# Strassen second layer from group 18 on in the first superblock, its operands prepared during the MLP

## The chip, the cores and the metric

The kernel runs on one core of one Trainium2 chip. The metric is the device time of one execution in microseconds (us). Five engines run their own instruction streams and wait for each other through semaphores: PE (matrix multiply; "PEld" is its loading of the stationary operand), DVE (VectorE), ACT (ScalarE), POOL (GpSimd) and SP, which here issues nearly all DMAs.

## The reference

Three blocks follow each other on 2304 tokens of width 512, all in fp32:

```
attention:  q_s = softmax(q), k_s = softmax over tokens (k);  x = q_s @ (k_s.T @ v)
MLP:        h = x @ w_in (512 -> 2048);  x = max(0.01 h, h) @ w_out (2048 -> 512)
experts:    P = exp(x @ w_gate - max), 8 rounds of row and column scaling (Sinkhorn)
            out = sum over 8 experts e of P[:, e] * (relu(x @ w1[e]) @ w2[e])    (512 -> 1024 -> 512)
```

Every expert is computed for every token, so the experts are the bulk of the work.

## The kernel before

**Numbers.** Each operand is kept as a high part in fp32r and a low part that is the rest; one product of two operands is three matmuls (high*high, high*low, low*high). The casts to the high part run on ACT, the subtractions that make the low part on DVE ("a split": lines L524 and L525).

**Stages.** Attention runs ahead of and beside the first MLP phase. The MLP has 4 phases of 4 units; each phase goes over 6 blocks of 384 tokens. One step is `first` (12 matmuls of 384 columns, into a bank `ph`) and `second` (12 matmuls into the four banks `y0` to `y3`). The program is written in half-steps: half-step 2s holds `first` of a later step, half-step 2s+1 `second` of step s. So the MLP has 192 half-steps of 12 matmuls; the last phase begins at half-step 144, the experts at 192. `at(t, f)` puts a task at half-step t. A task is a generator, and each `yield` hands over to the next half-step. `prep_half` makes the MLP's own weights for the next phase ready.

**Experts.** The tokens are 3 superblocks of 768. For each superblock 32 groups follow (a group is 256 hidden columns of one expert), 96 groups in all, numbered i = 0 to 95. A group has seven pieces, t0 to t6. Pieces t0 to t3 hold the first layer, which is Strassen's scheme in 7 products everywhere (42 matmuls of 384 columns, banks `pa` to `pd`). Pieces t4 to t6 hold the second layer of two groups back:

- In groups 2 to 33 that is the plain form: `y_tile`, 3 tiles of 12 matmuls of 512 columns, tokens as rows. DVE adds each tile to `acc` (line 743), scaled by P.
- From group 34 on it is Strassen's scheme, too: `y_pass`, 7 products, 42 matmuls of 384 columns, output columns as rows. The scaling by P is then done before it, on the hidden values, with rows of P that `p_load` fetches. ACT copies partial results into four temporary slots, POOL adds them (lines 804, 805). At a superblock's end `y_out` transposes the sums on PE and stores them.

**Where operands come from.** For groups 0 to 31 the weights are loaded raw, summed (POOL, DVE) and split (ACT, DVE), used from SBUF, and also stored: first layer to `d1` by `keep_w1`, second layer to `d2` by `keep` (lines 548 and 558). From group 32 on each operand (256 KB) is loaded from `d1` or `d2` into a ring of slots by `ring_load` (line 692), issued when the block 16 places ahead has been used. `x_ahead` and `x_next` sum and split the next superblock's inputs during the last groups of a superblock.

**Order.** PE, ACT, POOL and SP run in the order in which the program is written; DVE's order is chosen by a scheduler that knows no measured times. Each queue is strictly in order, so an instruction that waits holds up all behind it.

```
halves = ((0, 0), (1, 0), (0, 1), (2, 0), (1, 1), (3, 0), (2, 1), (3, 1))
for ph in range(1, NPH - 1):
    for n, (f, half) in enumerate(halves):
        at(H2 * ph + 4 + 4 * n, prep_half, PU * (ph + 1) + f, half)
at(T3 + 8, pair0)
```

Of the kernel before, what the change touches and what calls it, by code (L numbers as in the profile page):

```python
# [15 lines left out]
P = 128  # L16
# [6 lines left out]
def kernel(  # L23
# [60 lines left out]
    att_ctx, ml_ctx = ExitStack(), ExitStack()  # L84
# [26 lines left out]
    ml = ml_ctx.enter_context(tc.tile_pool(name="ml", bufs=2))  # L111
# [6 lines left out]
    def unit(u):  # L118
# [9 lines left out]
    halves0 = ((0, 0), (1, 0), (0, 1), (1, 1), (2, 0), (3, 0), (2, 1), (3, 1))  # L128
    queue = [
        (PU * ph + f, half) for ph in range(NPH) for f, half in (halves if ph else halves0)  # L130
    ]

    def load():
        if not queue:
            return
        u, half = queue.pop(0)
        t = raw_t[u, half] = ml.tile([P, 2 * DM], F32, tag="raw", name=f"raw{u}_{half}", bufs=3)
        nc.sync.dma_start(
            t.bitcast(U32), wm[u, :, half * DM : (half + 1) * DM].bitcast(U32)
        )  # L140

    def prep_half(u, half):
# [5 lines left out]
        a = ml.tile([P, DM], U32, tag="ca", name=f"ca{u}_{half}", bufs=3)  # L148
# [20 lines left out]
        load()  # L169
# [273 lines left out]
    WA = {"A11": 0, "A12": 1, "S3": 2, "A22": 3, "S1": 4, "S2": 5, "S4": 6}  # L443
    XB = {"B11": 0, "B22": 1, "T1": 2, "T3": 3, "T2": 4, "B21": 5, "T4": 6}
# [29 lines left out]
    def p_row(n):  # L474
        return mo((0, 3 * XS // 2)[n % 2], 2 * BLK).rearrange("p (t n) -> p t n", t=2)
# [38 lines left out]
    def pair_load(i):  # L514
        if i < NQ:
# [47 lines left out]
    def keep_w2(i):  # L563
        t = later["wb"][:, i % 3 * US : (i % 3 + 1) * US]
# [99 lines left out]
    def passes(i):  # L664

        if i < NQ + 2 or i == NG - 2:
            return ()
# [42 lines left out]
    def product(o, i, an, bn, start=True):  # L710

        assert ("xt", i // NQ, bn) in ready, (i, bn)
        if i < NQ:
# [5 lines left out]
    def y_tile(ph, tt):  # L719
# [24 lines left out]
        if e == E - 1 and half:  # L744
            nc.sync.dma_start(out[tt * P : (tt + 1) * P, :], a)
# [41 lines left out]
    def y_pass(g, dt):  # L787

        sb, first_, last = g // (NQ // 2), g % (NQ // 2) == 0, g % (NQ // 2) == NQ // 2 - 1
# [8 lines left out]
        def snap(b):  # L798
# [3 lines left out]
            t = acc[0][:, tmp_n[0] % 4 * BLK : (tmp_n[0] % 4 + 1) * BLK]  # L802
# [62 lines left out]
    def y_out(sb, dt, ya):  # L865
# [6 lines left out]
        for th, quads in enumerate(((c11, cc), (dd, c22))):  # L872
            for t in range(TB):
# [7 lines left out]
                o = acc[1][:, n % 6 * 2 * P : (n % 6 + 1) * 2 * P]  # L881
# [3 lines left out]
                    out[tok * P : (tok + 1) * P, :].rearrange("p (h t n) -> p h t n", h=2, t=2)[:, :, dt],  # L885
# [6 lines left out]
    def ends(i):  # L892
        return NQ < i < NG - 1 and i % NQ == NQ - 1

    def group(i):


        new = NQ <= i < NG
        g = i // 2 - 1
        pre = (g, i % 2 * TB) if 0 <= g < NQ // 2 else None  # L900
        nxt = w1_next(i)
        sec = i < NQ + 2
        if i < NG:
            bk = [bank(f"p{n}_{i}")[:, :BLK] for n in "abcd"]
            if i <= NQ:
# [21 lines left out]
        def second_ops(t):  # L927
# [11 lines left out]
            if half == 1 and i < NQ:  # L939
                if t < 2 and i > 1 and i + t < NQ:  # L940
# [5 lines left out]
        def t0():  # L946
# [13 lines left out]
            if i < NQ - 1:  # L960
# [332 lines left out]
```

## Time and profile before

| | |
|---|---|
| median of 3 runs | 1960.97 us (1960.8 to 1963.64) |
| profiled execution | 1961.5 us, span 1959.3 us |
| busy share of the span | PE 98%, PEld 95%, DVE 76%, ACT 41%, POOL 36% |
| mean granted TensorE clock | 0.996 of full speed |
| DMA | 430.43 MB, 220 GB/s over the span |

The span is from the first to the last instruction of the profiled execution; 2.2 us lie around it. A busy PE says only that matmuls were in flight. How fast they follow each other is read from their count in a stretch.

### The profile page before, as it was taken

The numbers are of one execution on the slowest core, as the hardware profiler recorded it, in microseconds if no ns is written. First come the engines' busy times: TensorE is split into PE (matmuls) and PEld (weight loads), VectorE is DVE, ScalarE is ACT, GpSimd is POOL, SyncE is SP. The second block draws the span as 40 slices with busy tenths as digits, with TensorE's granted clock in tenths as the row PEclk, the third lists the DMA queues.
The fourth block names the chain that finished last, engine by engine and source line by source line (L and its number), as shares of the span: only waits on it lengthen the run. The fifth ranks groups of instructions, "written<-read, shape, count | busy, mean of one in ns | idle before, by whom it ended". The sixth has DMA issues, their size and how long they took to land.

```text
span 1959.3 us, 30143 instructions
## 1 busy us (share of the span) xinstructions
PE 1928.8 (98%) x10739; PEld 1854.4 (95%) x10739; DVE 1493.9 (76%) x2212; ACT 803.1 (41%) x1480; POOL 709.3 (36%) x509
## 2 busy tenths in 40 slices
PE   7999999999999999999999999999999999999998
PEld 6999999999989999999989999999999999999998
DVE  7866535445788787887886888888898888888886
ACT  6754323233444444444434333333344433333333
POOL 4134212200133333343413445445633444544542
PEclk8999999999999999999999999999999999999999
DMA  6502111020588988889788887878888788888785
GB/s 241 169 13 80 59 33 53 24 70 1 176 312 279 331 288 302 314 296 326 264 295 310 260 259 262 260 235 279 252 257 269 249 263 261 260 262 261 253 260 152
DMA packets 237075, 430.43 MB, mean 220 GB/s; under 512 B 19952, under 2 KB 38528, under 8 KB 236928
## 3 DMA queue, kind: packets, MB, share of 16 engines
q1 hardware_dynamic: 236928, 428.51, 65.8%
q8 instruction: 87, 1.43, 0.3%
q14 instruction: 60, 0.49, 0.1%
HBM read 306.20 MB, written 122.23 MB: 219 GB/s over the span
## 4 chain that ended last, share of the span: by engine, by line
PE 43%; DVE 6%; issue 1%; ACT 1%; DMA 0%; SPq 0%; DVEq 0%; ACTq 0%
PE e L199 22%; PE pa L199 6%; PE pc L199 6%; PE pd L199 6%; PE pb L199 3%; DVE c L909 1%; DVE mo_t L783 1%; DVE xs L525 1%; DVE mo_t L769 1%; DVE wa L525 1%; DVE acc L810 0%; DVE acc L743 0%; ACT xs L524 0%; DVE wb_t L525 0%; DMA wa<-d 0%
## 5 line engine op out<-in xcount | busy, mean ns | idle before, releaser
L805 POOL TENSOR_TENSOR acc<-acc,acc 128x384 f32<-128x384 f32 x188 | 291.1, 1549 | 275.4 <-ACT acc L804 265.6
L199 PE MATMUL e<-xs,wb_t 128*128 128x384 f32 x1488 | 280.7, 334 | 1.2 <-ACT acc L882 0.7
L199 PE MATMUL e<-wb_t,xs 128*128 128x512 f32 x1152 | 268.5, 390 | 1.3 <-DVE rc L420 1.3
L199 PEld LDWEIGHTS e<-xs,wb_t 128*128 128x128 f32 x1488 | 259.7, 188 | 2.2 <-ACT acc L882 1.2
L199 PEld LDWEIGHTS e<-wb_t,xs 128*128 128x128 f32 x1152 | 215.5, 188 | 45.1 <-DVE rc L420 1.4
L525 DVE TENSOR_TENSOR wa<-mo_t,wa 128x768 fp32r<-128x768 f32 (+2 forms) x186 | 212.5, 1155 | 22.4 <-ACT wa L524 22.4
L199 PE MATMUL e<-wa,wb_t 128*128 128x384 f32 x1200 | 227.5, 334 | 0.9 <-issue 0.9
L783 POOL TENSOR_TENSOR mo_t<-mo_t 128x768 f32<-128x768 f32 x61 | 118.8, 1948 | 257.2 <-DVE mo_t L769 242.2
L199 PEld LDWEIGHTS e<-wa,wb_t 128*128 128x128 f32 x1200 | 209.6, 188 | 1.2 <-issue 1.2
L804 ACT COPY acc<-e 128x384 f32<-128x384 f32 x188 | 89.9, 480 | 262.1 <-PE e L199 262.1
L524 ACT CAST wa<-mo_t 128x768 fp32r<-128x768 f32 (+2 forms) x186 | 151.6, 843 | 79.0 <-DVE mo_t L783 59.0
L217 DVE TENSOR_TENSOR hh<-g,hh 128x384 fp32r<-128x384 f32 x96 | 61.4, 639 | 154.0 <-ACT g L216 154.0
L531 POOL TENSOR_TENSOR mo_t<-mo_t 128x256 f32<-128x256 f32 x32 | 29.3, 915 | 386.4 <-DVE wa L525 169.1
L199 PE MATMUL pa<-xs,wb_t 128*128 128x384 f32 x744 | 152.2, 339 | 1.7 <-ACT c L965 1.7
L525 DVE TENSOR_TENSOR xs<-mo_t,xs 128x768 fp32r<-128x768 f32 x127 | 136.9, 1094 | 21.6 <-ACT xs L524 21.6
L199 PE MATMUL pc<-xs,wb_t 128*128 128x384 f32 x744 | 149.0, 334 | 0.8 <-ACT c L990 0.8
L199 PE MATMUL pd<-xs,wb_t 128*128 128x384 f32 x744 | 149.3, 335 | 0.0
L810 DVE TENSOR_TENSOR acc<-e,acc 128x384 f32<-128x384 f32 x242 | 124.9, 548 | 27.8 <-PE e L199 17.4
L215 ACT ACTIVATE hh<-ph 128x384 fp32r<-128x384 f32 x96 | 47.3, 493 | 240.5 <-PE y L199 225.8
L199 PEld LDWEIGHTS pa<-xs,wb_t 128*128 128x128 f32 x744 | 129.0, 188 | 7.0 <-ACT c L965 6.2
L524 ACT CAST xs<-mo_t 128x768 fp32r<-128x768 f32 x127 | 103.1, 834 | 71.9 <-DVE mo_t L783 47.4
L199 PEld LDWEIGHTS pc<-xs,wb_t 128*128 128x128 f32 x744 | 130.7, 188 | 1.1 <-ACT c L990 1.1
(160 smaller groups left out, 3624.9 us busy)
## 6 DMA issues: line engine op xcount, KB each, us to landing
wb_t<-d SPq DMA_DIRECT2D x882, 256.0 KB, 3.2
d<-wa SPq DMA_DIRECT2D x32, 1792.0 KB, 9.4
d<-wb_t SPq DMA_DIRECT2D x90, 512.0 KB, 3.7
mo_t<-in_w SPq DMA_DIRECT2D x64, 512.0 KB, 6.6
raw<-in_wm SPq DMA_DIRECT2D x32, 512.0 KB, 3.7
d<-wa SPq DMA_DIRECT2D x22, 512.0 KB, 3.0
mo_t<-pd SPq DMA_DIRECT2D x32, 192.0 KB, 8.0
v<-in_vt SPq DMA_DIRECT2D x16, 320.0 KB, 5.7
```

What stands on the lines that cost most here:

```text
L199: nc.tensor.matmul(o, a, b, start=start, stop=stop, **more)
L215: nc.scalar.activation(hh[:, 0, :], p, AF.Prelu, alpha=0.01)
L217: nc.vector.tensor_tensor(hh[:, 1, :], g, r32(hh[:, 0, :]), op=ALU.subtract)
L524: nc.scalar.copy(hi, a)
L525: return lambda: nc.vector.tensor_tensor(lo, a, r32(hi), op=ALU.subtract)
L531: nc.gpsimd.tensor_tensor(s[:, 0], a21, a22, op=ALU.add)
L769: nc.vector.scalar_tensor_tensor(o, p, 0.0, r, op0=ALU.max, op1=ALU.mult)
L783: eng.tensor_tensor(raw_q(o), raw_q(x), raw_q(y), op=ALU.subtract)
L804: nc.scalar.copy(t, bk[b])
L805: nc.gpsimd.tensor_tensor(c22, c22, t, op=ALU.add)
L810: return nc.vector.tensor_tensor(a, bk[b], a, op=ALU.add)
L909: add = lambda o, x, y: nc.vector.tensor_tensor(o, x, y, op=ALU.add)
```

## The change

Groups 18 to 31 of the first superblock get the treatment of the later superblocks: `y_tile` ends with the second layer of group 17 (in groups 2 to 19), `y_pass` begins in group 20, and the ring of stored operands begins at group 18 instead of 32 (`N0 = 18`, `KP = 9`). For this the operands of groups 18 to 31 must be in DRAM before group 18. 28 tasks `early_op` (14 first-layer groups, 14 halves of second-layer pairs) make them during phases 1 to 3 of the MLP: each loads 512 KB raw three half-steps ahead (`early_load`), casts and subtracts (ACT, DVE) a part of 768 columns, does four additions of 256 columns on POOL, casts and subtracts a part of 1024 columns three half-steps later, and stores 768 KB and 1024 KB. The table `EARLY` holds their half-steps.

What comes with it: the MLP's raw weights are loaded three half-steps ahead, not as soon as a buffer is free, and `prep_half` moves to other half-steps. The preparation of groups 0 and 1 (`pair0`) moves from half-step 152 to 185 and 188. The plain part of the first superblock's sum is stored to `yp`, the Strassen part to `ys_` by a third use of `y_out`, with transposes; an accumulating DMA issued on POOL adds them in DRAM (`y_sum`, group 37), and `y_done` copies the result to the output two groups later. `acc[4]` and `acc[5]` are saved to DRAM at the start of the experts and loaded back in group 44, to make room for temporaries.

```
+    N0 = 18
+    KP = N0 // 2
...
-        if i < NQ + 2 or i == NG - 2:
+        if i < N0 + 2 or i == NG - 2:
             return ()
...
-        if i < NQ:
+        if i < N0:
             block(o, chunk("a", i % 2 * 7 + WA[an]), xt(bn), start)
...
+        o = early_out(3, at_)
+        part(o, t[:, 1:])
+        yield
+        put(o, 0, 3)
+        a21, a11, a12, a22 = (t[:, k] for k in range(4))
+        nc.gpsimd.tensor_tensor(a22, a21, a22, op=ALU.add)
+        nc.gpsimd.tensor_tensor(a21, a11, a21, op=ALU.subtract)
+        nc.gpsimd.tensor_tensor(a11, a22, a11, op=ALU.subtract)
...
+        yield
+        yield
+        o = early_out(4, at_ + 3)
+        part(o, t)
+        yield
+        put(o, 3, 4)
...
+    EARLY = (
+        53, 57, 61, 65, 69, 73, 78, 83,
+        94, 98, 102, 106, 110, 114, 118, 124, 131,
+        149, 152, 155, 158, 161, 164, 167, 170, 173, 176, 179,
+    )
...
-        for n, (f, half) in enumerate(halves):
-            at(H2 * ph + 4 + 4 * n, prep_half, PU * (ph + 1) + f, half)
-    at(H2 * (NPH - 1) - 4, open_pairs)
+        for t, (f, half) in zip((5, 11, 16, 21, 28, 33, 39, 44), halves2):
+            at(H2 * ph + t - 3, load, True)
+            at(H2 * ph + t, prep_half, PU * (ph + 1) + f, half)
+    at(H2 * (NPH - 1) + 2, open_pairs)
...
-    at(T3 + 8, pair0)
-    at(T3 + 26, second_load, 0)
+    for n, t in enumerate(EARLY):
+        at(t - 3, early_load, n)
+        at(t, early_op, n, t)
+    for i in range(2):
+        at(END - 11 + i, pair_load, i)
+        at(END - 7 + 3 * i, pair_first, i)
...
+        if i == NQ + 5:
+            for th in range(2):
+                at(t + th, y_sum, th)
+                at(t + 14 + th, y_done, th)
```

`early_out` picks where a prepared part lies until it is stored: of three or four free places in `wa`, `wb` or `xs` the one that was used longest ago.

**ACT, in the last MLP phase.** These rows stand on ACT before, around the splits of the experts' inputs (`xs<-acc`, lines 361 and 524); `hh` and `g` are the two forms of the MLP's hidden values that a later `second` needs, and the numbers in names tell buffers apart.

```order
L524 CAST xs<-acc_80 128x768
L524 CAST xs<-mo_t 128x768
L215 ACTIVATE hh_4207<-ph_4194 128x384
L216 ACTIVATE g_4208<-ph_4194 128x384
L524 CAST xs<-acc_80 128x768
L361 CAST xs<-acc_81 128x768
L215 ACTIVATE hh_4245<-ph_4232 128x384
L216 ACTIVATE g_4246<-ph_4232 128x384
```

At the same place now (L536 and L365 are the old L524 and L361, L219 and L220 the old L215 and L216, L1206 is `early_op`'s cast):

```order
L536 CAST xs<-acc_80 128x768
L536 CAST xs<-mo_t 128x768
L219 ACTIVATE hh_4498<-ph_4485 128x384
L220 ACTIVATE g_4499<-ph_4485 128x384
L536 CAST xs<-acc_80 128x768
L1206 CAST wa<-mo_t 128x4x256
L1206 CAST xs<-mo_t 128x3x256
L365 CAST xs<-acc_81 128x768
L219 ACTIVATE hh_4548<-ph_4535 128x384
L220 ACTIVATE g_4549<-ph_4535 128x384
```

Two casts of raw operands now stand ahead of the next hidden values; each waits for a load from DRAM or for POOL's sums, and for the store that last read its target.

**SP, in the last MLP phase.** Before, the last raw MLP weights (L138) are followed at once by the loads for the first groups (L517, L521) and then by the stores of group 0 and later (L548, L558):

```order
L138 DMA raw_0_3187<-in_wm 128x1024
L138 DMA raw_1_3267<-in_wm 128x1024
L138 DMA raw_1_3339<-in_wm 128x1024
L517 DMA mo_t<-in_w 128x2x512 x4
L521 DMA mo_t<-in_w 128x2x512
L548 DMA d_0_104<-wa 128x7x512
```

Now loads of `early_load` (L1169, L1170, L1175) alternate there with stores of `early_op` (L1210) for the whole phase; this is one stretch of it:

```order
L1175 DMA mo_t<-in_w 128x4x128
L1175 DMA mo_t<-in_w 128x2x128 x2
L1210 DMA d_13_152<-wa 128x4x512
L1210 DMA d_27_134<-wa 128x3x512
L1169 DMA mo_t<-in_w 128x512
L1170 DMA mo_t<-in_w 128x2x256
L1210 DMA d_27_134<-wa 128x4x512
L1210 DMA d_13_152<-xs 128x3x512
```

Each store waits on DVE, and the loads written behind it wait with it; the last phase had no store before.

**DVE, where the ring begins.** Before, that is from group 31 to 32. These rows are DVE's there: seven splits of the next superblock's inputs (L525 with `xs`, six of them here) stand among the tile sums (L743), the first layer's sums (L909) and hidden values (L750):

```order
L525 TENSOR_TENSOR xs<-mo_t,xs 128x768
L909 TENSOR_TENSOR c_31_8605<-pd_8603,c_31_8605 128x384
L750 SCALAR_TENSOR_TENSOR xs<-c_31_8605,xs 128x384
L525 TENSOR_TENSOR xs<-mo_t,xs 128x768
L743 SCALAR_TENSOR_TENSOR acc_80<-e_3_8687,pm,acc_80 128x512
L525 TENSOR_TENSOR xs<-acc_81,xs 128x768
L525 TENSOR_TENSOR xs<-acc_82,xs 128x768
L743 SCALAR_TENSOR_TENSOR acc_80<-e_4_8705,pm,acc_80 128x512
L525 TENSOR_TENSOR xs<-acc_82,xs 128x768
L525 TENSOR_TENSOR xs<-t_1_8606,xs 128x768
L525 TENSOR_TENSOR wb_t<-mo_t,wb_t 128x2x4x128
L743 SCALAR_TENSOR_TENSOR acc_80<-e_5_8722,pm,acc_80 128x512
```

Now it is from group 17 to 18 (L537, L777, L784, L945 are the old L525, L743, L750, L909):

```order
L945 TENSOR_TENSOR c_17_7210<-pd_7208,c_17_7210 128x384
L784 SCALAR_TENSOR_TENSOR xs<-c_17_7210,xs 128x384
L537 TENSOR_TENSOR wb_t<-mo_t,wb_t 128x2x4x128
L777 SCALAR_TENSOR_TENSOR acc_80<-e_3_7281,pm,acc_80 128x512
L777 SCALAR_TENSOR_TENSOR acc_80<-e_4_7295,pm,acc_80 128x512
L784 SCALAR_TENSOR_TENSOR xs<-c_17_7209,xs 128x768
L777 SCALAR_TENSOR_TENSOR acc_80<-e_5_7309,pm,acc_80 128x512
```

The splits of inputs have left this place, since the superblock doesn't change there; they stand at the end of group 31 as before, where the ring now runs already.

## Rows read from the trace of the kernel before

**Rows 1.** The page: busy engines, and the span in 40 slices.
```profile
PE 1928.8 (98%) x10739; PEld 1854.4 (95%) x10739; DVE 1493.9 (76%) x2212; ACT 803.1 (41%) x1480; POOL 709.3 (36%) x509
PE   7999999999999999999999999999999999999998
GB/s 241 169 13 80 59 33 53 24 70 1 176 312 279 331 288 302 314 296 326 264 295 310 260 259 262 260 235 279 252 257 269 249 263 261 260 262 261 253 260 152
```

**Rows 2.** Stretches: PE, PEld, DVE, ACT, POOL busy us (instructions), granted clock, DMA share, GB/s.
```profile
799.49:923.54 124.05, 124.05 (x625) 112.49 (x624) 100.35 (x137) 55.31 (x88) 45.24 (x40) 1.00 0.86 305
923.54:985.57 62.03, 62.03 (x314) 56.24 (x312) 52.33 (x68) 28.59 (x47) 26.83 (x20) 1.00 0.73 261
985.57:1020.39 34.82, 31.75 (x158) 28.00 (x156) 30.85 (x42) 13.19 (x20) 7.05 (x4) 1.00 0.95 353
1020.39:1137.30 116.91, 116.91 (x673) 116.37 (x672) 91.08 (x123) 45.96 (x82) 45.77 (x29) 1.00 0.83 276
1400.34:1538.48 138.14, 135.43 (x781) 133.51 (x781) 116.94 (x159) 59.72 (x111) 53.59 (x36) 1.00 0.83 257
```

**Rows 3.** Waits of PE over the span: us in total, times, longest.
```profile
PE pc L199 <- DMA wa<-d: 3.1, 2, 1.9
PE pa L199 <- ACT c L965: 1.7, 2, 1.2
PE y L199 <- ACT acc L236: 1.6, 2, 1.3
```

**Rows 4.** Timeline of SP in group 32: start, us.
```profile
995.97 1.11 SPq L692 DMA_DIRECT2D wa<-d  x2
1001.82 0.34 SPq L745 DMA_DIRECT2D out<-acc  x1
...
1002.69 3.03 SPq L692 DMA_DIRECT2D wa<-d  x5
```

**Rows 5.** Timeline of DVE at the same time.
```profile
997.15 1.58 DVE L525 TENSOR_TENSOR wa<-mo_t,wa 128x512 fp32r<-128x512 f32 x1
...
1001.05 0.74 DVE L743 SCALAR_TENSOR_TENSOR acc<-e,pm,acc 128x512 f32<-128x512 f32 x1
```

**Rows 6.** Stretches of the MLP and of groups 0 to 4, columns as in rows 2.
```profile
142.00:192.00 50.00, 48.45 (x275) 47.81 (x275) 37.38 (x48) 22.27 (x48) 22.27 (x15) 1.00 0.24 74
...
295.40:396.50 101.10, 101.10 (x580) 101.10 (x579) 48.11 (x89) 29.56 (x65) 23.94 (x20) 1.00 0.12 37
396.50:496.40 99.90, 99.89 (x573) 95.05 (x572) 48.13 (x74) 35.91 (x69) 6.95 (x8) 1.00 0.10 35
...
496.40:564.40 68.00, 65.66 (x344) 59.04 (x343) 56.30 (x111) 34.05 (x58) 18.32 (x18) 1.00 0.70 240
```

**Rows 7.** Groups of DVE's instructions by line and shape, last MLP phase.
```profile
L217 DVE TENSOR_TENSOR hh<-g,hh 128x384 fp32r<-128x384 f32 x22 | 12.6, 573 | 48.0 <-ACT g L216 48.0
L238 DVE TENSOR_TENSOR acc<-y,acc 128x384 f32<-128x384 f32 x24 | 12.4, 554 | 2.9 <-PE y L199 2.8
L525 DVE TENSOR_TENSOR wa<-mo_t,wa 128x1024 fp32r<-128x1024 f32 x2 | 2.4, 1220 | 0.0
L525 DVE TENSOR_TENSOR wa<-mo_t,wa 128x768 fp32r<-128x768 f32 x2 | 1.9, 953 | 0.2 <-ACT wa L524 0.2
```

**Rows 8.** The same of ACT.
```profile
L215 ACT ACTIVATE hh<-ph 128x384 fp32r<-128x384 f32 x21 | 10.3, 492 | 61.8 <-PE y L199 61.8
L524 ACT CAST wa<-mo_t 128x1024 fp32r<-128x1024 f32 x2 | 2.1, 1052 | 0.0
L524 ACT CAST wa<-mo_t 128x768 fp32r<-128x768 f32 x2 | 1.7, 840 | 0.0
```

**Rows 9.** The page: costliest groups, of POOL.
```profile
L805 POOL TENSOR_TENSOR acc<-acc,acc 128x384 f32<-128x384 f32 x188 | 291.1, 1549 | 275.4 <-ACT acc L804 265.6
L531 POOL TENSOR_TENSOR mo_t<-mo_t 128x256 f32<-128x256 f32 x32 | 29.3, 915 | 386.4 <-DVE wa L525 169.1
```

**Rows 10.** The page: DMA issues, KB each, median us to landing.
```profile
d<-wa SPq DMA_DIRECT2D x32, 1792.0 KB, 9.4
...
mo_t<-in_w SPq DMA_DIRECT2D x64, 512.0 KB, 6.6
```

**Rows 11.** Stretches of 10 us with full DMA engines, columns as in rows 2.
```profile
700.00:710.00 10.00, 10.00 (x51) 8.86 (x50) 7.50 (x10) 4.67 (x7) 2.63 (x4) 1.00 1.05 393
...
1010.00:1020.00 10.00, 10.00 (x48) 8.63 (x48) 9.86 (x13) 3.38 (x5) 2.04 (x1) 1.00 1.05 403
```

**Rows 12.** Groups of DVE's instructions, half-steps 29 to 53 of the MLP.
```profile
L217 DVE TENSOR_TENSOR hh<-g,hh 128x384 fp32r<-128x384 f32 x12 | 12.7, 1056 | 9.6 <-ACT g L216 9.6
...
L152 DVE TENSOR_SCALAR ca<-ca 128x512 f32<-128x512 f32 x7 | 8.0, 1147 | 2.0 <-ACT ca L150 2.0
```

More of the change, by code (lines that the diff above doesn't have):

```diff
@@ L128, with load @@
     halves0 = ((0, 0), (1, 0), (0, 1), (1, 1), (2, 0), (3, 0), (2, 1), (3, 1))
+    halves2 = ((0, 0), (1, 0), (0, 1), (1, 1), (2, 0), (2, 1), (3, 0), (3, 1))
     queue = [
-        (PU * ph + f, half) for ph in range(NPH) for f, half in (halves if ph else halves0)
-    ]
-    def load():
-        if not queue:
+        (PU * ph + f, half)
+        for ph in range(NPH)
+        for f, half in (halves2 if ph > 1 else halves if ph else halves0)
+    ]
+    def load(free=False):
+        if queue[0][0] >= 2 * PU and not free:
             return
         u, half = queue.pop(0)
-        t = raw_t[u, half] = ml.tile([P, 2 * DM], F32, tag="raw", name=f"raw{u}_{half}", bufs=3)
+        t = raw_t[u, half] = later["ml"].tile([P, 2 * DM], F32, tag="raw", name=f"raw{u}_{half}", bufs=later["raws"])
         nc.sync.dma_start(
@@ L147, in prep_half @@
         hi, lo = unit(u)[:, half, 0, :], unit(u)[:, half, 1, :]
-        a = ml.tile([P, DM], U32, tag="ca", name=f"ca{u}_{half}", bufs=3)
+        a = later["ml"].tile([P, DM], U32, tag="ca", name=f"ca{u}_{half}", bufs=6 - later["raws"] if later["raws"] == 3 else 1)
         af, ef = a.bitcast(F32), w1.bitcast(F32)
@@ L637, with x_away, x_back, y_sum @@
     x_parts = {}
+    def x_away():
+        for k in range(2):
+            nc.sync.dma_start(xd[k], acc[2 * NSB - 2 + k])
+    def x_back():
+        for k in range(2):
+            nc.sync.dma_start(acc[2 * NSB - 2 + k], xd[k])
+    def y_sum(th):
+        rows = slice(th * BLK, (th + 1) * BLK)
+        nc.gpsimd.dma_start(yp[rows, :], ys_[rows, :], accum_op=ALU.add, max_dma_last_dim=4 * DM)
+    def y_done(th):
+        rows = slice(th * BLK, (th + 1) * BLK)
+        nc.sync.dma_start(out[rows, :], yp[rows, :])
+    def stage_y(sb, n):
+        return acc[2 * NSB - 1 if sb == 0 else 1][:, n % 6 * 2 * P : (n % 6 + 1) * 2 * P]
     def x_ahead(sb):
@@ L743, in y_tile @@
             nc.vector.scalar_tensor_tensor(a, y, scale, a, op0=ALU.mult, op1=ALU.add)
-        if e == E - 1 and half:
-            nc.sync.dma_start(out[tt * P : (tt + 1) * P, :], a)
+        if ph == KP - 1:
+            nc.sync.dma_start(yp[tt * P : (tt + 1) * P, :], a)
     def relu_split(i, th, u, p):
@@ L787, in y_pass @@
     def y_pass(g, dt):
-        sb, first_, last = g // (NQ // 2), g % (NQ // 2) == 0, g % (NQ // 2) == NQ // 2 - 1
+        sb, last = g // (NQ // 2), g % (NQ // 2) == NQ // 2 - 1
+        first_ = g == KP or g % (NQ // 2) == 0
+        tmp = acc[2 * NSB - 2 if g < NQ // 2 + 4 else 0]
         ya = [
@@ new lines, with early_out @@
+    out_used = {"s": 0, 0: 0, 1: 0, 2: 0}
+    out_n = [0]
+    def early_out(m, t):
+        ph, r = t // H2, t % H2
+        if ph == NPH - 1:
+            ks = (0, 1, 2)
+        else:
+            ks = (3, 2) if r < 26 else (3,)
+        a = wa if ph % 2 else later["wb"]
+        where = {k: a[:, k * US : (k + 1) * US] for k in ks}
+        if m == 3:
+            where["s"] = xs[:, 12 * XS : 13 * XS]
+        k = min(where, key=lambda k: out_used.get(k, 0))
+        out_n[0] += 1
+        out_used[k] = out_n[0]
+        return where[k][:, : m * OW]
@@ L1122, with open_raws @@
+    def open_raws():
+        ml_ctx.close()
+        later["ml"] = ml2_ctx.enter_context(tc.tile_pool(name="ml2", bufs=2, reuse_waits="tile"))
+        later["raws"] = 4
     x0 = []
```

152 lines of the change are left out of this document (95 added, 57 removed).

## The prediction

> **What bounds the kernel now.** I read the page first: PE is busy for 98% of the span and in 38 of 40 slices for nine tenths or more, while DVE stands at 76% and POOL at 36% [rows 1]. So time can go only where PE has fewer or faster matmuls, or waits less. Next came the stretches, where the reader is to divide time by count. Groups 20 to 27 (plain second layer) take 124.05 us for 8 x 78 matmuls, that is 15.51 us a group; groups 34 to 41 (Strassen) take 116.91 us for 8 x 84, that is 14.61 us, both at granted clock 1.00 and with PE never idle [rows 2]. From the second, 384 columns cost 174 ns; put into the first, 512 columns cost 228 ns. Last, the waits: no wait of PE totals more than 3.1 us after the front of the program, and the two that matter here are one on a DMA into `wa` and one of `y` on ACT [rows 3]. The experts are paced by matmul issue, and so is the MLP: 101.10 us for 580 matmuls, 2.09 us a half-step, with DMA at 37 GB/s [rows 6]. The change takes PE work from groups 20 to 33 and puts vector and DMA work under the MLP, which has room for it.
>
> **The sum.** It is made against the profiled execution of 1961.5 us, which is 0.5 above the median.
>
> *Groups 20 to 27* become like 34 to 41: 124.05 to 116.91, **-7.1 us** [rows 2].
>
> *Groups 28 to 36* become like 60 to 68, which hold the same things at the next change of superblock: `x_ahead` on POOL, `x_next`, `y_out` with 24 transposes on PE, the waits that these bring. Before: 62.03 + 34.82 us for groups 28 to 33, and three groups at 14.61, together 140.69. After: 138.14, all waits included [rows 2]. **-2.5 us**. So of the 14 groups that get cheaper (14 x 0.89 = 12.5 us), the new boundary gives some 6.5 back, and 3.8 lost at the old place (34.82 against 2 x 15.51) drops out of this line.
>
> *Groups 18 and 19* get the start of the ring, which cost that 3.8 us in groups 32 and 33. Where did it come from? SP stood from 997 to 1001.8 us at a store of `acc`, and only then, at 1002.69, issued the five ring loads for which PE waited [rows 4]; the store waited for DVE's tile sum, which started at 1001.05, behind a split stretched to 1.58 us and others [rows 5]. DVE was late since seven splits of the next superblock's inputs (0.95 us each [rows 7], 6.7 us) stood in its queue from group 31. These are not at the new place, as the order of DVE's rows shows; everything else is. With the tile sum some 4 us earlier, the ring loads go out in time. I take **+0.5 us**, bounds 0 and 3.8.
>
> *The MLP.* Each of the 28 tasks adds 1.22 + 0.95 us on DVE [rows 7], 1.05 + 0.84 on ACT [rows 8] and 4 x 0.92 on POOL [rows 9]. The last phase has 11: DVE goes from 48 to 72 us of 100, ACT from 36 to 57, POOL from 7 to 47; in the phase before, with nine, DVE goes from 48 to 68, ACT from 30 to 47, POOL from 24 to 57 [rows 6]. No engine becomes the bound: in groups 20 to 27 DVE had 81% and PE lost nothing [rows 2]. So only the order can hurt, through two slacks. Hidden values: their two forms are written from the end of `second(s)` and read three half-steps later, 6.27 us less 2 x 0.49 and 0.57 [rows 7, 8], so ACT may stand still for 4.7 us. Result banks: `y0` is complete 9 matmuls before `second` ends and needed 12 after, so DVE's 0.55 us sum [rows 7] may be 3.7 us late. Behind a waiting `early_op` cast stand ACT's next hidden values, and behind its subtraction on DVE those bank sums. A load goes out 6.27 us ahead, so it must take longer than 6.27 + 3.7 = 10 us before PE notices; loads land after 6.6 us and even stores of 1792 KB after 9.4 with DMA queues nearly full [rows 10]. Below, the loss may be -1.6, if the moved `prep_half` ends the one wait of `y` on ACT there [rows 3]. Above, the nearest is the stretch at 142 us, where POOL at 45% stretched DVE and PE lost 1.55 of 50 us [rows 6]; over three phases that is 9.3. I take **+2.5 us**, nearer to the window at 295 us, where nothing was lost, since that wait at 142 us was one on ACT's copies of first results, which exist only in the first phase.
>
> *The start of the experts.* The two `pair_first` put four splits (4.3 us of DVE) and eight POOL sums just ahead of group 0, out of the middle of the phase. In groups 0 to 4 DVE is busy 56.3 of 68.0 us and PE loses 2.3 [rows 6]. **+0.5 us**, bounds 0 and 2.3 (as much again).
>
> *The sum in DRAM and the rest.* No accumulating DMA and no DMA from POOL is in the trace. Its cover is `y_done`, two groups (29 us) later; that copy waits on SP ahead of ring loads, which are themselves 16 blocks (16.7 us) ahead of PE. By the nearest row, 1792 KB in 9.4 us [rows 10], the two sums of 768 KB, counted as read, read and written, need some 25 us: inside. If POOL stood still as long, its adds from four temporary slots, six in 14.6 us, would stop after 10 us, and PE could lose 15. POOL is 39% busy there [rows 2], and issuing costs SP a third of a us [rows 4]; I take **+0.3 us**, bounds 0 and 15. The Trainium skill ("DMA: Bandwidth & Descriptors", section on the SWDGE path) gives a DMA from GpSimd 2.0 us plus bytes over 436 GB/s, an estimate of 3.8 us each, which would be hidden and leave the sum as it is; no run here shows it yet. At nothing I cost: saving and loading back `acc[4]`, `acc[5]` (3 MB, DMA share 0.70 and 0.83 there [rows 2, 6]; cost if not hidden: the ring's delay beyond 16.7 us), the six `yp` stores (they replace six output stores), and `p_load` a group later (14.6 us still ahead).
>
> Together -7.1 - 2.5 + 0.5 + 2.5 + 0.5 + 0.3 = -5.9 us (unrounded -7.14 and -2.55): 1955.6 for a profiled execution, **1955.1 us** as a median, 0.3% faster.
>
> **A rule beside the row.** 512 columns measure 228 ns and 384 measure 174, from rows 2. The Trainium skill ("TensorE: Matmul & The Clock Gate", section "Back-to-back issue gap") has columns over 2.4 GHz plus 2.5 ns, 215.8 and 162.5, each 12 ns less than the rows. By it a pair of groups saves 72 x 215.8 - 84 x 162.5 = 1.89 us instead of 1.78, and the sum would end 0.7 us lower. I keep the rows: a fixed cost per matmul speaks against a scheme with more and shorter matmuls, and the rows contain it.
>
> **Rivals.**
>
> *DMA too slow in the last phase.* There 11 tasks move 11 x 2.36 = 25.9 MB in 33 half-steps (69 us), 376 GB/s, where now 35 go. For it: no slice of the page is over 331 [rows 1]. At that rate the tasks need 78.4 us and end 9.4 late; 3.7 are slack, 5.7 reach PE: 1961 us. Against it: 10 us stretches ran at 393 and 403 GB/s [rows 11]. 15%.
>
> *DVE and POOL disturb each other: slower.* For it: at 142 to 192 us `hh` took 1056 ns where it takes 573 [rows 7, 12], with POOL at 45%; the new POOL load in phases 1 and 2 is above that. The loss decides where it eats the other terms, at 8.4 us, near the 9.3 of that stretch's rate kept up over three phases. At twice the rate over phases 1 and 2, 12.4 us: 1965 us. Against it: `prep_half` is spread over 44 half-steps now, not 19, and groups 34 to 41 have POOL at 39% and DVE at 78% with no loss [rows 2]. 10%. The Trainium skill ("GPSIMD Engine Reference", section 1) says that GpSimd shares its SBUF interfaces with VectorE, with contention for DVE instructions with two SBUF inputs; the row of `hh`, 1056 ns, agrees.
>
> *The boundary costs more*, through POOL held by the accumulating DMAs: +7 us, half the bound, 1962 us. Only the missing rows speak for it. 7%.
>
> *All is hidden*: no MLP loss, none at the start of the experts, none at groups 18 and 19, so that the first two terms stand alone: 1961.0 - 9.7 = 1951 us. 13%.
>
> **From this the numbers.** My forecast, 1951.5 to 1958.5, has 55%. What tells from no change is about 0.2%, here 3.9 us: below 1957.0 is faster, above 1964.9 slower. Faster: most of the forecast (50%), the last rival, and a mild form of the others, 66%. Same: the rest of the forecast, the DMA case, most of the boundary case, 23%. Slower: 11%. The range 1950.5 to 1961.5 reaches to the DMA case and the hidden one.
>
> **What would show it.** Right: groups 20 to 27 at 14.6 us each with DMA near 275 GB/s; a boundary at groups 28 to 36 of some 138 us with two short waits; no wait of PE on DMA at groups 18 and 19; the three MLP phases a few us over 2.09 us a half-step; the last one near 376 GB/s with DVE at about 72%. Wrong: PE waits on `ACT g`, `DVE hh` or `DVE acc` all through the MLP, loads of `early_load` landing after 10 us, POOL silent for 10 us around the accumulating DMAs, or ring loads late behind `y_done`.

## The result and the profile after

The changed kernel takes 1989.27 us (median of 4 runs, 1987.82 to 1991.03), the kernel before 1961.25 beside it: a ratio of 1.0141, 95% interval 1.0123 to 1.0158. It is 28 us slower where 6 us faster had been forecast. The profiled execution took 1989.16 us with a span of 1986.2.

The page of the changed kernel: busy time of TensorE and GpSimd, then TensorE, its granted clock and the traffic in 40 slices.

```profile
PE 1933.6 (97%) x10847; PEld 1870.7 (94%) x10847; DVE 1571.6 (79%) x2260; ACT 837.3 (42%) x1533; POOL 826.7 (42%) x606
PE   7999999998999999999999999999999999999998
PEclk8999999999999999999999999999999999999999
GB/s 241 169 15 65 249 217 273 212 145 284 247 303 278 299 323 281 310 294 263 253 251 275 300 269 299 257 263 260 253 252 267 258 261 261 261 256 242 274 259 153
```

Against [rows 1] the traffic of slices 5 to 10 is the new thing (145 to 284 GB/s where 1 to 70 went), and TensorE is under nine tenths in the last of them. So the question is the MLP. The stretches of the changed kernel (columns as in [rows 2]): three of the MLP, one piece of the first, then groups 20 to 27 and 28 to 36 of the experts.

```profile
189.00:289.00 100.00, 94.15 (x516) 92.10 (x515) 70.76 (x97) 41.95 (x77) 49.43 (x46) 0.97 0.72 230
289.00:390.00 101.00, 96.02 (x535) 94.27 (x534) 68.59 (x94) 41.36 (x76) 56.25 (x52) 0.98 0.72 239
390.00:528.00 138.00, 128.18 (x705) 120.50 (x704) 87.05 (x120) 61.47 (x106) 52.75 (x55) 0.98 0.66 216
244.91:251.73 6.82, 6.09 (x18) 5.55 (x19) 5.22 (x9) 2.63 (x4) 6.18 (x5) 0.50 0.83 285
836.20:953.13 116.93, 116.93 (x672) 116.39 (x673) 93.13 (x120) 44.55 (x81) 53.75 (x32) 1.00 0.86 283
953.13:1091.29 138.16, 135.43 (x782) 133.51 (x781) 117.00 (x159) 59.73 (x111) 53.62 (x36) 1.00 0.82 262
```

The last two rows are the experts, and they came out as forecast to a tenth of a us: 116.93 us for groups 20 to 27 (forecast 116.91) and 138.16 for groups 28 to 36 (138.14). The first three are the loss. At 189 us TensorE issues 516 matmuls in 100 us, where the MLP of before had 580 in 101.10 [rows 6]. The fourth row is a piece of the first in which the granted clock was 0.50, its lower level of 1.2 GHz, just after a wait of 2.52 us (below). There were four such falls in the MLP, at 244.91 (6.83 us), 357.55, 456.54 and 500.91 (3.41 each). Together that is 17.1 us at half clock; as an estimate, half of it, some 8.5 us, is lost. The first matmul of group 0 is issued at 528.1 us, where it was at 496.4 [rows 6]: 31.7 us lost in the MLP, 4.8 of them won back behind it (the spans differ by 26.9).

What TensorE waited for from 142 to 528 us in the changed kernel (us in total, times, longest):

```profile
PE y L203 <- DVE acc L242: 12.9, 11, 2.5
PE pg L203 <- DVE xs L366: 6.2, 5, 1.9
PE y L203 <- ACT acc L240: 1.5, 2, 1.2
```

Before, the MLP had only the last of these, 1.6 us [rows 3]. The new ones are for VectorE: its bank sums, line 242, and, half as long, the split of the experts' inputs, line 366. How the sums come late is seen just ahead of the longest wait, in the timeline of the changed kernel (start, duration, engine, line; in brackets the idle time before it and what ended it).

```profile
237.59 1.30 POOL L169 TENSOR_TENSOR ca<-ca,wa 128x512 f32<-128x512 f32 x1
237.67 1.05 ACT L1206 CAST wa<-rawe 128x1024 fp32r<-128x1024 f32 x1 [4.22 <-POOL rawe L1226]
...
238.75 1.23 DVE L1207 TENSOR_TENSOR wa<-rawe,wa 128x1024 fp32r<-128x1024 f32 x1 [3.35 <-ACT wa L1206]
238.97 2.17 POOL L170 TENSOR_TENSOR wa<-ca,raw 128x512 fp32r<-128x512 f32 x1
...
239.90 1.66 DVE L221 TENSOR_TENSOR hh<-g,hh 128x384 fp32r<-128x384 f32 x1
...
242.68 0.95 DVE L1207 TENSOR_TENSOR wa<-rawe,wa 128x768 fp32r<-128x768 f32 x1
...
244.15 0.55 DVE L242 TENSOR_TENSOR acc<-y,acc 128x384 f32<-128x384 f32 x1
...
244.84 1.56 PE L203 MATMUL y<-hh,wb_t 128*128 128x384 f32 x4 [2.52 <-DVE acc L242]
```

Two things can be read here. ScalarE's second cast of an operand stood 4.22 us for GpSimd's sums (line 1226), and VectorE's subtraction behind it 3.35 us. And the small subtraction of line 221, 0.57 us in [rows 7], took 1.66 us beside GpSimd's line 170, which itself took 2.17 (lines 169 and 170 prepare the MLP's own weights, as lines 166 and 167 did before). Which of the two costs the time can't be seen from a timeline; the experiments are about that.

### The profile page after: what moved, and what is told of

Same layout as the page of the kernel before. It is cut to its first block, busy times and chain, and to the rows that moved or that the text cites. A ratio compares the mean times of both kernels' runs of the same rounds, so it can differ in the third digit from the quotient of the medians.

```text
span 1986.2 us, 31354 instructions
## 1 busy us (share of the span) xinstructions
PE 1933.6 (97%) x10847; PEld 1870.7 (94%) x10847; DVE 1571.6 (79%) x2260; ACT 837.3 (42%) x1533; POOL 826.7 (42%) x606
## 4 chain that ended last, share of the span: by engine, by line
PE 49%; DVE 7%; issue 1%; ACT 1%; DMA 1%; SPq 0%; ACTq 0%; DVEq 0%
PE e L203 25%; PE pa L203 7%; PE pc L203 7%; PE pd L203 7%; PE pb L203 3%; DVE c L945 2%; DVE mo_t L817 1%; DVE mo_t L803 1%; DVE wa L537 1%; DVE xs L537 1%; DVE acc L846 1%; DMA wb_t<-d 0%; ACT xs L536 0%; PE po L915 0%; ACT acc L918 0%
## 5 line engine op out<-in xcount | busy, mean ns | idle before, releaser
L841 POOL TENSOR_TENSOR acc<-acc,acc 128x384 f32<-128x384 f32 x228 | 350.2, 1536 | 342.7 <-ACT acc L840 330.7
L203 PE MATMUL e<-xs,wb_t 128*128 128x384 f32 x1884 | 351.6, 335 | 2.9 <-ACT acc L918 1.4
L203 PEld LDWEIGHTS e<-xs,wb_t 128*128 128x128 f32 x1884 | 328.3, 188 | 4.6 <-ACT acc L918 2.5
L203 PE MATMUL e<-wa,wb_t 128*128 128x384 f32 x1392 | 262.6, 334 | 0.0
L537 DVE TENSOR_TENSOR wa<-mo_t,wa 128x768 fp32r<-128x768 f32 (+2 forms) x164 | 196.2, 1208 | 15.9 <-ACT wa L536 15.9
L203 PE MATMUL pa<-xs,wb_t 128*128 128x384 f32 x912 | 186.6, 339 | 4.6 <-ACT c L1001 2.9
L537 DVE TENSOR_TENSOR xs<-mo_t,xs 128x768 fp32r<-128x768 f32 x158 | 168.2, 1086 | 28.9 <-ACT xs L536 28.9
L203 PE MATMUL pd<-xs,wb_t 128*128 128x384 f32 x912 | 183.2, 335 | 0.0
L536 ACT CAST wa<-mo_t 128x768 fp32r<-128x768 f32 (+2 forms) x164 | 134.1, 841 | 99.2 <-DVE mo_t L817 75.5
L536 ACT CAST xs<-mo_t 128x768 fp32r<-128x768 f32 x158 | 127.8, 834 | 91.5 <-DVE mo_t L817 55.4
L203 PEld LDWEIGHTS pd<-xs,wb_t 128*128 128x128 f32 x912 | 160.0, 188 | 0.2 <-DVE c L945 0.2
L203 PE MATMUL e<-wb_t,xs 128*128 128x512 f32 x648 | 153.0, 394 | 1.3 <-DVE rc L424 1.3
L817 DVE TENSOR_TENSOR mo_t<-mo_t 128x768 f32<-128x768 f32 x82 | 149.1, 1820 | 0.0
L203 PEld LDWEIGHTS e<-wb_t,xs 128*128 128x128 f32 x648 | 122.2, 190 | 26.4 <-DVE rc L424 1.4
```

The lines of the kernel that those rows point to most:

```text
L203: nc.tensor.matmul(o, a, b, start=start, stop=stop, **more)
L536: nc.scalar.copy(hi, a)
L537: return lambda: nc.vector.tensor_tensor(lo, a, r32(hi), op=ALU.subtract)
L817: eng.tensor_tensor(raw_q(o), raw_q(x), raw_q(y), op=ALU.subtract)
L841: nc.gpsimd.tensor_tensor(c22, c22, t, op=ALU.add)
```

## The experiments

**Theory A**: the chain of each operand (ScalarE's cast, VectorE's subtraction, GpSimd's four sums, ScalarE's second cast three half-steps later) is too long, and ScalarE, in order, stands. **B**: it is the work that VectorE and ScalarE got. **C**: loads and stores are late. **D**: GpSimd's sums hold up VectorE's operations. Differences below are of medians, to the kernel before on the same chip; the change itself stands 28.0 us over it.

**e1, the second cast later.**

```diff
-        yield
-        yield
-        o = early_out(4, at_ + 3)
+        gap = 5 if at_ >= T3 else 6 if at_ % H2 < 33 else 3
+        for _ in range(gap - 1):
+            yield
+        o = early_out(4, at_ + gap)
```

> The second cast of an operand is issued 6 half-steps (5 in the last phase) after the first instead of 3, nothing else. Theory A (ScalarE stands in order behind that cast, which waits for GpSimd's four sums): ScalarE's waits for GpSimd fall from about 41 us to under 10, the MLP gives back 18 to 28 of the 31.7 us it lost, 1962 to 1972 us. Rival B (it is the work itself that VectorE and ScalarE got, wherever it is issued): 1984 to 1992. Rival C (loads and stores are late or slow): within 3 us of 1989.

1983.33 us, ratio 1.0108 (1.0093 to 1.0123): 7 us better than the change, not 18 to 28. ScalarE's waits for GpSimd from 189 to 515 us in the changed kernel were, the four largest:

```profile
ACT wa L1206 <- POOL mo_t L1226: 15.8, 5, 4.8
ACT wa L1206 <- POOL rawe L1226: 9.4, 3, 4.2
ACT wa L1206 <- POOL rawe L1224: 9.0, 3, 4.1
ACT wb_t L1206 <- POOL rawe L1224: 4.0, 2, 3.1
```

and in this run, with one wait of TensorE among them:

```profile
ACT ca L153 <- POOL wa L170: 5.8, 2, 3.5
...
PE y L203 <- ACT wa L1206: 5.1, 1, 5.1
...
ACT wb_t L1206 <- POOL rawe L1224: 3.8, 2, 3.1
...
ACT wa L1206 <- POOL rawe L1220: 1.4, 1, 1.4
```

For the second cast some 5 us were left of about 41, but the MLP still lost 27 (group 0 at 523.7 us). The later cast changed the order on ScalarE, too: TensorE stood 5.1 us once for a cast of line 1206 (the second line shown). So A as forecast here fails; how small its part is, this run doesn't tell. B's 1984 is as near.

**e2, without the sums.** The four `nc.gpsimd.tensor_tensor` of `early_op` are deleted.

> GpSimd's four sums of each of the 28 operands are left out (the stored operands are then not those that the experts need); casts, subtractions, loads and stores stay. Theory A: no cast waits for a sum, 1958 to 1970 us. Rival D (GpSimd's sums slow VectorE, with which they share the reading of SBUF): the same time, and VectorE's subtractions of 1.5 k columns get shorter by tenths of a us; only the first run tells A from D. Rival B: 1980 to 1989. Rival C: within 3 us of 1989.

1963.16 us, 1.0004 (0.9995 to 1.0013). GpSimd's sums are the loss, 27 us of the 28; loads, stores, casts and subtractions together cost little.

**e3 and e4, traffic alone, and nothing.** In e3 the two instructions of `part` go as well, and a memset fills the buffer that a store would read unwritten; in e4 `early_load` and `early_op` are not planned, and the ring reads other operands:

```diff
-            ring += [d1[i % NQ][place_of(i % NQ >= N0)[n]] for n, _ in FIRST]
+            ring += [d1[i % NQ % N0][place_of(i % NQ >= N0)[n]] for n, _ in FIRST]
...
-        at(t - 3, early_load, n)
-        at(t, early_op, n, t)
+        pass
```

(the same for `d2`).

> Of the 28 operands only the loads and stores stay: no casts, subtractions or sums (what is stored is whatever stands in the buffers). Theories A, B and D: the MLP is as long as before to about 3 us, 1953 to 1959 us. Rival C: most of the 31.7 us stays, 1975 to 1989.

> Nothing of the 28 operands is made in the MLP; the experts read operands of other groups in their place, so the traffic there is the same and the values are wrong. Every theory: the time that the experts' part of the change is worth by itself, before minus 9.7 plus 2 to 5 for their start: 1953 to 1957 us. If it is over 1960, the loss is not in the making of the operands but in the MLP's changed loads and preparation.

e3: 1959.08 us, 0.9982 (0.9973 to 0.9992). e4: 1956.76, 0.9969 (0.9959 to 0.9980). C falls. With e2 the loss comes apart, each as difference to before: nothing made -5.7 us; loads and stores +2.3, to -3.4; casts and subtractions +4.1, to +0.7; sums +27.3, to +28.0. The stretches of e4, which have the changed loads and preparation of the MLP's own weights, show nothing lost by those:

```profile
189.00:289.00 100.00, 98.89 (x565) 98.89 (x566) 47.95 (x90) 30.72 (x67) 23.95 (x18) 1.00 0.19 59
289.00:389.00 100.00, 100.00 (x573) 100.00 (x572) 45.68 (x88) 29.44 (x64) 20.11 (x17) 1.00 0.09 27
```

**e5, sums that nothing waits for.**

```diff
-        nc.gpsimd.tensor_tensor(a22, a21, a22, op=ALU.add)
...
+        for _ in range(4):
+            nc.gpsimd.tensor_tensor(scr, a11, a12, op=ALU.add)
```

> GpSimd does four sums of the same size per operand at the same place, but reads only and writes to a buffer of its own: nothing waits for them (the stored operands lack the real sums). Theory A (the wait of ScalarE's second cast for the sums): that wait is gone, so 1960 to 1968 us, as without sums (1963.2). Theory D (GpSimd's sums hold up VectorE's operations of two SBUF operands, above all the low part of the hidden values, line 221, 0.56 us alone and 1.0 us on average beside a GpSimd sum): the loss stays in the main, 1977 to 1989 us, with line 221 still at 0.75 to 0.85 us on average.

1986.05 us, 1.0119 (1.0104 to 1.0134): the sums cost 22 us although no engine waits for them. This run had no wait of ScalarE for a sum, and VectorE's line 221 and TensorE's waits still read:

```profile
L221 DVE TENSOR_TENSOR hh<-g,hh 128x384 fp32r<-128x384 f32 x79 | 60.9, 771 | 87.4 <-ACT g L220 87.4
```

```profile
PE y L203 <- DVE acc L242: 12.0, 9, 3.7
PE pg L203 <- DVE xs L366: 4.8, 5, 2.2
```

So most of the loss needs no wait for a sum: that decides against A as the main cause, and for D. (That a GpSimd which is merely busy would do the same is not excluded until e17.)

**e6, the hidden value in PSUM.** VectorE's groups in the changed kernel from 142 to 515 us (line, tiles and shapes, count, busy us, mean ns) are

```profile
L221 DVE TENSOR_TENSOR hh<-g,hh 128x384 fp32r<-128x384 f32 x79 | 65.6, 831 | 81.2 <-ACT g L220 81.2
L242 DVE TENSOR_TENSOR acc<-y,acc 128x384 f32<-128x384 f32 x66 | 33.5, 547 | 2.2 <-PE y L203 2.2
...
L155 DVE TENSOR_SCALAR ca<-ca 128x512 f32<-128x512 f32 x23 | 15.9, 691 | 3.0 <-ACT ca L153 3.0
```

Both of the first two subtract or add 384 columns. Line 242 reads one operand from PSUM and takes 547 ns; line 221 reads two from SBUF and takes 831. Taken one by one from the same trace, 35 of line 221's operations have no GpSimd operation beside them (overlapping by more than 0.01 us) and take 0.556 us on average; 43 have one and take 1.06, up to 1.68. Of line 242's, 11 without and 55 with one take 0.548 and 0.547. So the edit gives line 221 what line 242 has:

```diff
-        g = hp_.tile([P, BLK], F32, tag="g", name=f"g{s}", bufs=1)
...
-        nc.scalar.activation(g, p, AF.Prelu, alpha=0.01)
-        nc.vector.tensor_tensor(hh[:, 1, :], g, r32(hh[:, 0, :]), op=ALU.subtract)
+        nc.scalar.activation(p, p, AF.Prelu, alpha=0.01)
+        nc.vector.tensor_tensor(hh[:, 1, :], p, r32(hh[:, 0, :]), op=ALU.subtract)
```

> The MLP's hidden value is kept in its PSUM bank instead of in SBUF before VectorE subtracts the high part from it: line 221 then has one SBUF operand, as line 242 has, which stays at 0.55 us beside GpSimd. Everything else as after. Theory D, if the stretch of line 221 is what hurts: line 221 at 0.55 to 0.6 us, the MLP gives back 8 to 20 us, 1969 to 1981 us. Theory A: within 3 us of 1989. If D holds but it is the sum over all of VectorE's operations that hurts: 1981 to 1987.

1974.46 us, 1.0061 (1.0046 to 1.0076): 11.1 us over before, so 17.0 of the 28.0 are won back (14.8 by the two medians; 14.1 in the MLP, where group 0 begins at 514.0 instead of 528.1), by an edit that removes no work. It also does away with the single buffer `g`, but ScalarE had stood only 0.9 us for that in the changed kernel. The line, now 220:

```profile
L220 DVE TENSOR_TENSOR hh<-ph,hh 128x384 fp32r<-128x384 f32 x81 | 44.8, 553 | 90.1 <-ACT ph L219 90.1
```

**e7, the sums on VectorE** (`nc.gpsimd` becomes `nc.vector` in the four sums).

> The four sums are made by VectorE instead of GpSimd: no wait of ScalarE for GpSimd, no sums beside VectorE, but 112 more operations of about 0.35 us there (about 40 us). Theory D: 1966 to 1980 us, since VectorE loses about as much to the stretch now. Theory A: 1962 to 1970. Rival B (VectorE is simply too full for the half-step that its operations have): 1990 to 2005.

1983.23 us, 1.0098 (1.0083 to 1.0113), just above D's range. A sum takes 0.42 us on VectorE where nothing holds it, but now bank sums stand behind the sums themselves:

```profile
PE y L203 <- DVE acc L242: 14.6, 11, 4.7
```

The sums' hold is gone and 30 us of work have come in its place (VectorE 229.8 us busy from 189 to 490 us, 199.8 in e2). So work given to VectorE costs time, too. That work alone does it is not shown: ahead of the 4.7 us wait, lines 165 and 221 took 1.75 and 1.67 us beside GpSimd's lines 169 and 170, 0.69 and 0.56 alone.

**e8, both edits.**

> The later second cast and the hidden value in PSUM together. If both A and D are real the gains add: 1958 to 1972 us. If D alone counts: the same as the hidden value in PSUM alone, to 3 us.

1975.69 us, 1.0065 (1.0048 to 1.0082), the same as e6. The later cast adds nothing once line 221 is free of the hold, though here, too, TensorE stood once for a cast (line 1205), 3.2 us.

**e9, hidden value in PSUM and no sums.**

> The hidden value in PSUM, and GpSimd's four sums left out (the stored operands lack them). If the 18 us that the hidden value in PSUM leaves are the sums' hold on VectorE's other operations (theory D goes on): 1957 to 1962 us, the time with no operands made (1956.8) plus 1 to 5. If they are the casts and subtractions themselves (rival B): 1966 to 1973.

1961.97 us, 0.9996 (0.9986 to 1.0006), at the upper end of D's range. So with line 221 safe the sums still cost some 12 us (12.5 by the medians, 11.9 by the differences to before). Its stretches and those of e6 show that it isn't VectorE's busy time (e9 first):

```profile
189.00:289.00 100.00, 99.31 (x568) 98.99 (x567) 64.89 (x105) 45.51 (x84) 27.77 (x18) 1.00 0.75 242
```

```profile
189.00:289.00 100.00, 97.33 (x544) 96.11 (x543) 60.29 (x98) 42.84 (x79) 50.36 (x48) 0.98 0.75 242
```

**e10, other times.** With the hidden value in PSUM, `EARLY` is 53, then pairs at 57, 58, 65, 66, ... (first half-steps after a block's bank sums), from 149 on 153, 154, 161, 162, ...

> The hidden value in PSUM, and the 28 operands begun two by two at the first half-steps after the four bank sums (line 242) of a block have to be done, so that none of their work stands ahead of bank sums on VectorE. If what is left is bank sums that come late behind the operands' work: TensorE's waits for them fall from 6.6 us to under 3 and the time to 1964 to 1971 us. If it is VectorE's total: 1972 to 1977.

1989.16 us, 1.0137 (1.0121 to 1.0152), worse than either theory said. The pairs ran out of output buffers, and ScalarE waited for stores:

```profile
ACT wa L1205 <- DMA d<-wa: 23.4, 6, 5.3
ACT wb_t L1205 <- DMA d<-wb_t: 17.8, 4, 6.0
```

The run says nothing on whether the bank sums are what is left.

**e11, ten groups instead of fourteen** (`N0 = 22`, 20 operands, hidden value in PSUM; `EARLY` is 57, 61, 65, 73, 77, 82, 97, ... 177).

> The hidden value in PSUM, and only the operands of the last 10 groups made early (20 instead of 28, one in 4 to 8 half-steps), the experts' switch at group 22 instead of 18. The experts gain less (about 3.5 us of 7.1 for the groups 20 to 27 go), the MLP loses less: if the loss goes with the number of operands 1971 to 1974 us, if it grows faster than their number 1962 to 1969.

1973.26 us, 1.0053 (1.0038 to 1.0068). With fewer operands gain and loss shrink together, as the first of the two forecasts had it; a loss that grows faster than their number is not seen.

**e12 and e16, the kernel before with the hidden value in PSUM.**

> The kernel before with the hidden value in PSUM and nothing else. By theory D there is little to win, as GpSimd has only the weights' preparation there and 6 of 71 of line 221's operations meet it: 1958 to 1963 us.

> The kernel before with the hidden value in PSUM, timed again: 0.9979 to 0.9998 of before in the first timing. If the gain is real the interval lies under 1 again, 1959 to 1962 us; the profile's first stretch of the MLP shows it as 0.6 us less lost.

1960.75 us, 0.9988 (0.9979 to 0.9998), and again 1962.28 us, 1.0000 (0.9992 to 1.0009). The first interval's gain did not come back; no difference is shown.

**e13, e14, e15: what are the 12 us?** All with the hidden value in PSUM. e13 has e5's sums, e14 cuts the operands of the sums to 32 columns (`t[:, k, :32]`), e15 is e4.

> The hidden value in PSUM, and GpSimd's sums as in e5: as long as the real ones, at the same place, but nothing waits for them. If the 12.5 us left are the sums' hold on VectorE's other operations: 1970 to 1977 us, as with real sums (1974.5). If they are ScalarE's waits for the sums: 1960 to 1965, as without sums (1962.0).

> The hidden value in PSUM, and the sums on 32 of their 256 columns (the other columns of the stored operands lack them): the chain from cast to subtraction to sums to the second cast stays, GpSimd's time in it falls to about a quarter. Hold on VectorE: 1962 to 1967 us. Waits of ScalarE in a chain: these fall too, so 1964 to 1970; only together with e13 does this run tell.

> The hidden value in PSUM, none of the 28 operands made (the experts read others in their place). The ceiling of the change: 1954 to 1957 us, 0 to 3 us under the same without the hidden value in PSUM (1956.8).

e13: 1976.71 us, 1.0075 (1.0060 to 1.0091). e14: 1962.61, 0.9999 (0.9990 to 1.0008). e15: 1956.08, 0.9966 (0.9954 to 0.9978). Sums that nobody waits for cost at least as much as real ones, short ones that are waited for cost nothing. GpSimd does hold VectorE's other operations, such as line 155 above (0.691 us on average; 0.424 where no GpSimd operation stands beside it), although it reads only one operand from SBUF.

But that this is all of e6's 12 us is not shown. The traces give the time that VectorE is held beside the sums from 142 to 515 us, over all its operations (each one's duration less the median of its kind with nothing of GpSimd beside it): 5 us in e6, where ScalarE still stands 34 us for the sums, and 14 us in e13, where it stands for none. So the two can lose the same time for different reasons, and e14 takes both away at once. Against Theory A in e6 speaks e8, which leaves 4 of the 34 us and gains nothing; but there the held time rises to 9 us.

**e17, a GpSimd that only writes.**

```diff
+        for _ in range(12):
+            nc.gpsimd.memset(scr, 0.0)
```

in place of the sums, with the hidden value in SBUF as in the change.

> The four sums of an operand are replaced by twelve memsets of 128 x 256 on GpSimd into a buffer of its own, some 3 to 4 us in all at the same place: GpSimd is as busy, but reads nothing (the stored operands lack the sums). If it is the reading that holds VectorE's second operand: line 221 beside GpSimd's memsets stays at 0.56 us and the time is that without sums, 1960 to 1967 us. If GpSimd's running alone does it: as with sums that nothing waits for, 1980 to 1989 us.

1963.06 us, 1.0003 (0.9993 to 1.0012). GpSimd is busier than in the changed kernel (the fifth busy time of a row), and TensorE is as busy as without sums (99.0 and 97.2 in e2):

```profile
189.00:289.00 100.00, 97.90 (x558) 97.26 (x557) 69.73 (x104) 45.13 (x84) 56.38 (x113) 1.00 0.76 242
289.00:389.00 100.00, 97.89 (x555) 96.62 (x554) 66.53 (x103) 42.73 (x78) 58.05 (x124) 1.00 0.73 245
```

Line 221 took 0.60 us on average beside a memset (33 operations from 189 to 490 us): 0.555 in the 29 that had a memset alone beside them, and only the other four had line 169 or 170 there as well. So what holds VectorE is that GpSimd's sums read SBUF, not that GpSimd runs.

## Why the prediction was wrong

**Right, but for their start: the experts.** Groups 20 to 27 and 28 to 36 are exact, because their price was read from groups of the same kind. Group 19 lost 1.9 us to one wait of 1.7 us on a ring load (forecast 0.5 for groups 18 and 19, bounds 0 and 3.8). The start of the experts lost about 3 us more than before in groups 1 and 4 (forecast 0.5, bound 2.3), half of that through one more fall of the clock, 3.41 us at 593 us. The sum in DRAM cost nothing (forecast 0.3). Its DMAs in the changed kernel are below (queue, count, KB each, median us to landing). The accumulating one, from GpSimd's queue, took three times the 3.8 us that the prediction estimated from the Trainium skill ("DMA: Bandwidth & Descriptors", section on the SWDGE path), and was hidden all the same:

```profile
yp<-ys POOLq DMA_DIRECT2D x2, 768.0 KB, 12.9
out<-yp SPq DMA_DIRECT2D x2, 768.0 KB, 7.0
```

**Failed: the MLP, forecast +2.5 us, measured +31.7.** The step that failed is "No engine becomes the bound ... So only the order can hurt, through two slacks". It added up durations and looked only for late loads; e3 shows the loads harmless. But a duration on VectorE is not fixed when GpSimd reads SBUF beside it, and the 28 operands' sums, which the prediction counted as load on POOL alone, cost 27 us (e2). With nothing waiting for a sum they still cost 22 (e5), and a GpSimd as busy that only writes costs nothing that shows (e17). One of the prediction's own signs of being wrong came of it, TensorE's waits for `DVE acc`: 12.9 us in 11 waits. In the changed kernel 43 operations of line 221 took 0.5 us longer, 22 us in all, on the engine on which the bank sums stand in order.

These 22 us are not all the sums' own. 26 of the 43 operations stood beside sums (7 us); 17 stood beside lines 169 and 170 (15 us). Without the sums, in e2, the preparation still held line 221 for 7.9 us, at no loss that shows. So the slacks do hide such delays up to a point. Where that point lies was not measured, and the held times don't add up to the loss. One of the two slacks was also stated too wide: 21 matmuls of 0.174 us are 3.7 us, but the sum's own 0.55 comes off, which leaves 3.1.

**The right mechanism was a rival, at 10% and too cheap.** "DVE and POOL disturb each other" was priced by TensorE's loss at 142 to 192 us, 1.55 us in 50, kept up over three phases (9.3), and 12.4 at its worst. The price per operation stood in the trace of before: of line 217's 81 operations from 142 to 515 us, 9 met GpSimd and took 1.31 us, up to 1.67, and in [rows 12] the mean is 1056 ns. With the change 43 met it instead of 9, and four of the waits in the MLP, of 1.6 to 2.5 us, were each followed by a fall of the clock within 1.2 us.

**The evidence against that rival was no evidence.** "Groups 34 to 41 have POOL at 39% and DVE at 78% with no loss" [rows 2] does not mean that nothing was held there. The bank sums of that window (line 810, `acc<-e,acc`) read PSUM and took 0.55 us with and without GpSimd beside them, but line 783, two operands of SBUF, took 2.17 us with it (six operations) and 0.95 in the one without. TensorE just didn't wait for those. The changed kernel shows the same at 960 to 1090 us: line 846, the old 810, takes 0.544 us without and 0.551 with, line 537 0.95 and 1.37. A share of busy time says neither what the operations read nor how soon TensorE needs their results.

**On the wait for GpSimd,** which the trace after shows most plainly (41 us of ScalarE): e1 and e5 take most or all of it away and win 7 and 5 us, e8 wins nothing over e6. In each of these VectorE's time held beside sums grew, though (to 22, 31 and 9 us, from 16, 16 and 5), so what the wait costs by itself was not separated. It is not the main part, since e5 loses 22 us without it.

The Trainium skill ("SBUF — State Buffer", section "Who interferes with whom") states the rule: a VectorE instruction with two SBUF inputs contends with a GpSimd instruction that reads SBUF, not with one that only writes, and the lock on the shared ports is exclusive. The runs agree on each part: 1.06 against 0.556 us for line 221, 0.547 for line 242 with PSUM, 0.555 beside memsets alone. And of the 34 operations of line 221 that began in the changed kernel while a GpSimd operation had more than 0.15 us to go, 33 ended 0.41 to 0.42 us after it, while the five that had begun 0.07 to 0.16 us ahead of a sum kept 0.55 to 0.56. The page gives no price for a chain of engines; that took these runs.

**What stays open.** How the 17 us that e6 wins divide between later hidden values and later bank sums was not separated, nor how the 12 it leaves divide between the hold on other operations and ScalarE's waits. Nor was it shown why e7's 30 us of work on VectorE cost 19 us of time, where the casts' and subtractions' 60 us (from e4 to e2 in the same stretch, 139.1 to 199.8) cost 4; that the load has a knee between 66% and 76% is a guess.

**No version that makes its operands beats the kernel before.** The ceiling of the change is 6.6 us (e15). The traffic of the operands takes 2.3 and their casts and subtractions 4.1, so even sums that cost nothing end at before (e2, 1.0004; e14, 0.9999).

## What to carry to other kernels

When work is given to an idle GpSimd, ask of VectorE's operations on the critical path how many operands they read from SBUF, and look in the trace for the same operation with and without a GpSimd operation beside it: its longest duration, less the undisturbed one, is the price, its count after the change the quantity. That bounds what is held, not what TensorE loses: 7.9 us held on line 221 cost nothing in e2. Counting operands isn't enough either, as line 155 with one operand from SBUF was held, too. Here an operand left in PSUM took line 221 out of the contention for no added work. And a window that "lost nothing at the same load" is evidence only if the same kind of operation stands on the path in it, with as little slack.

## What was not expected of the hardware

GpSimd busy with memsets for 56 and 58 us of 100 cost no more than a GpSimd without sums (TensorE 97.9 us busy in both, 99.0 and 97.2 in e2), where with sums, GpSimd at 49 and 56, TensorE stood 5.9 and 5.0 us in 100 and 101. The contention runs both ways: GpSimd's sums of 128x256 took 0.74 us with nothing of VectorE beside them and up to 1.4 with it. And four waits of TensorE of 1.6 to 2.5 us were followed by 3.4 to 6.8 us at a granted clock of 0.50, so, by estimate, some 8.5 us of the loss were paid in slower matmuls behind the waits.
